# Where the gates of an output projection stand in an attention block on one Trainium2 core, with two roundings on GpSimd and two stores on ScalarE's queue

## The chip, the core and the metric

The kernel runs on one core of a Trainium2 chip. The core has five engines, each with its own queue of instructions, executed in order: TensorE (PE, with PEld for its weight loads), VectorE (DVE), ScalarE (ACT), GpSimd (POOL) and SyncE (SP, which here only issues transfers). An engine that meets an instruction whose input is not there waits, and everything behind it on that engine waits too. Metric is the device time of one execution in microseconds (us). Before the change it is 1550.36 us (median of three runs, 1550.10 to 1550.55).

## The reference

`x` is 2048 tokens by 512 channels. It is normalised by row; one branch is attention with 32 heads of 16 channels and an output projection `wo`, the other a two-layer network whose output passes through SiLU; the result is `x + s * g`.

```
xn = layernorm(x)
q, k, v = split(xn @ wqkv)                 # 32 heads of 16
p = softmax(q @ k.T * 16**-0.5)
s = concat_heads(p @ v) @ wo
h = gelu(xn @ w1 + b1) @ w2 + b2
g = silu(h)                                # = 0.5 * h * (1 + tanh(h / 2))
out = x + s * g
```

All is float32. Products that need the accuracy are made of three matrix multiplications of rounded parts: a number is split into a high part (rounded, `oh`, `wo_h`) and the rest (`ol`, `wo_l`), and high x high, low x high and high x low are added up in PSUM.

## The kernel before

The first part of the program makes the projections and the second branch; it writes `h` to DRAM as `g_d`. The main part is a list of 512 **steps**, n = 0 to 511, and a step 512 that closes it. Head groups (8 of 4 heads) and query chunks (4 of 512 tokens) make 32 units of 16 steps. A step takes 128 keys: four matrix multiplications of scores (`T` in the order strings, line 714, banks `ps`, `two` twice, `pst`), their three exponentials on ScalarE (lines 717 and 719), and the multiplication with the values (`V`, line 785, bank `pv`). Up to step 492 the steps also hold the row maxima of later units (`S`, `X`, `Y`: line 193 on TensorE, line 199 on VectorE).

From step `DONE = 493` the maxima are over, and their three PSUM banks (`ps_a`, `ps_b`, `ps_x`, handed out in turn by `s_tile`) serve the output projection, the **Wo part**. It takes tokens in blocks of 128. Blocks 0 to 9 go in **pairs** (0,1), (2,3) ... (8,9), each pair in four steps n to n+3, with n = 493, 497, 501, 505, 509. For a pair there are:

- `load_gx` (lines 841, 842): `g_d` and `x` of a block into `gx`, by SyncE's queue;
- `w_two` (lines 884 to 896), twice for a pair: 128 x 512 values of the attention output are rounded to `oh` (line 890 on ScalarE, or 892 on GpSimd), and GpSimd makes `ol` (line 893);
- `w_halves` (line 912, `H` in the order strings): the multiplications with `wo`, eight pieces in four steps. The pair's first piece needs two banks; of the three, one is free, and the other is that of the first block of the pair before;
- `gate` (lines 844 to 847): tanh on ScalarE into a scratch tile, then `g * (1 + tanh)` on VectorE, in place in `gx`. Scratch tile is number t % 4 of `home(0)`, so blocks 2 and 10, 4 and 12, 6 and 14 share one;
- `w_out` (`W` in the order string, step n+3): `w_gate` on VectorE (line 918) multiplies the bank with the gate and so frees the bank, `w_add` on GpSimd (line 923) adds `x`, and a transfer on SyncE's queue stores the block.

Blocks 10 to 15 (`late`) only get their gates there, one at every second step from 499 on; their projection follows after the last step. There the last unit's output is divided by its softmax sums: `os` is copied from PSUM, `dr` (the sums) is fetched from it, its reciprocal goes to DRAM (`den_d`, line 814), comes back spread over the rows (`dn`, line 817), and `o_div` multiplies (line 823). Then come the last rounding and the last multiplications.

The order of each engine's queue is the order in which the program is recorded: step by step, in a step by the letters of `ORDER` or `TWO`, and what `at(n, f, ...)` has put on a step is recorded behind its last `T`. Two steps of the Wo part run `TTTTHH` (odd n) and `HTTTTHWV` (even n).

Of the kernel before, what the change touches and what calls it, by code (L numbers as in the profile page):

```python
# [16 lines left out]
P = 128  # L17
# [37 lines left out]
def fused(ctx: ExitStack, tc: tile.TileContext, x, wqk, wv, wo, w1, b1, w2, b2, out):  # L55
    nc = tc.nc
# [254 lines left out]
    for j in range(len(pairs)):  # L311
        for h in range(2):
# [9 lines left out]
            n = 2 if nd < len(parts) and parts[nd][2] and ready - nd > room else 1  # L322
            n = max(n, need - 2 * (left - 1))
# [496 lines left out]
    def o_div(u, eng):  # L820
        g, c = divmod(u, NCH)
        rs = slice(64 * (g % 2), 64 * (g % 2) + 64)
        eng.tensor_mul(ot[c][rs, g // 2], ot[c][rs, g // 2], DN.pop(u)[rs])

    GX, OTS, PW, homes = {}, {}, {}, {}
# [23 lines left out]
    def w_round(blocks, src, lo):  # L849
        if blocks == [(t, KT - 1) for t in T3]:  # L850
            both = slot(3 + len(PN) % 3, (P, 4, KT, P), F32R)
            oh, ol = both[:, 0], both[:, 1]
        else:
            oh = wb.tile([P, KT, P], F32R, name="oh", bufs=3)
            ol = wb.tile([P, KT, P], F32R, name="ol", bufs=3)
        n = len(blocks)
        nc.scalar.activation(oh[:, :n], src, AF.Copy)
        lo.tensor_sub(ol[:, :n], src, oh[:, :n].bitcast(F32))
        for i, b in enumerate(blocks):
            OTS[b] = (oh[:, i], ol[:, i])  # L860
# [5 lines left out]
    def w_chunk(k, lo):  # L866
        w_round([(t, k) for t in T3], ot[NCH - 1][:, k].rearrange("p (t s) -> p t s", s=P), lo)

    def cols(t):
        n = 2 if t == NT - 1 else 1  # L870
        return [slice(i * D // n, (i + 1) * D // n) for i in range(n)]

    def w_mul(t, ks, parts=(0, 1)):
        if t not in PW:
            PW[t] = [t_bank(3 if t == NW else 2 if t == NW + 1 else 1) if NW <= t < NT - NCH or i else
                     ps_m.tile([P, CH], F32, name="ps") if t == NT - 1 else s_tile()[0]
                     for i, cs in enumerate(cols(t))]
        for i, cs in enumerate(cols(t)):
            if i in parts:
                for k in ks:  # L880
                    mm3(PW[t][i][:, :cs.stop - cs.start], OTS[t, k], (wo_h[:, k, cs], wo_l[:, k, cs]),
                        k == 0, k == KT - 1)

    def w_two(t, k0):
        oh, ol = [wb.tile([P, KT, P], F32R, name=x, bufs=3) for x in ("oh", "ol")]
        c, i = divmod(t, NCH)
        src = ot[c][:, k0:k0 + 2, i * P:(i + 2) * P]
        hi, lo = [w.rearrange("p (k t) s -> p k (t s)", t=2) for w in (oh, ol)]
        if t or k0:
            nc.scalar.activation(hi, src, AF.Copy)  # L890
        else:
            nc.gpsimd.tensor_copy(hi, src)
        nc.gpsimd.tensor_sub(lo, src, hi.bitcast(F32))
        for k in range(2):
            for j in range(2):
                OTS[t + j, k0 + k] = (oh[:, 2 * k + j], ol[:, 2 * k + j])
# [24 lines left out]
    def w_add(t, eng, i=0):  # L921
        gx, cs = GX[t], cols(t)[i]
        eng.tensor_add(gx[:, 0, cs], gx[:, 0, cs], gx[:, 1, cs])
        nc.sync.dma_start(out[t * P:(t + 1) * P, cs], gx[:, 0, cs])

    def w_out(t, eng):
        w_gate(t)
        w_add(t, eng)
# [3 lines left out]
    def at(n, f, *a, pos=3):  # L932
        todo.setdefault((n, pos), []).append((f, a))
# [27 lines left out]
    late = range(NW, NT)  # L961
    for t in range(NW):
        n = DONE + 4 * (t // 2)
        at(n - 3 + t % 2, load_gx, t)
        if t % 2 == 0:
            for i in range(2):
                at(n + i - 2, w_two, t, 2 * i)
            for i in range(4):
                for j in range(2):
                    at(n + i, w_halves, t, i % 2 * 2 + j, i // 2, pos="H")  # L970
        at(n + t % 2, gate, t)
        at(n + 3, w_out, t, nc.gpsimd, pos="W")
    for i, t in enumerate(late):
        n = L - 2 * len(late) - 1 + 2 * i
# [10 lines left out]
    for n in range(L + 1):  # L985
        ua, ka = divmod(n, 16)
        want = due(n) - due(n - 1)
        i = 0
# [42 lines left out]
            w_mul(t, (k,))  # L1031
    o_div(NU - 1, nc.vector)
    w_chunk(KT - 1, nc.vector)
    for t in T3[:2]:
        w_mul(t, KS[2:3])
    ends = [(t, i) for t in T3 for i in range(len(cols(t)))]
    for n, (t, i) in enumerate(ends):
        w_mul(t, KS if t == NT - 1 else KS[2:] if t == T3[2] else KS[3:], (i,))
        w_gate(t, i)
        w_add(t, nc.vector, i)  # L1040
# [33 lines left out]
```

## Time and profile before

| | |
|---|---|
| median of three runs | 1550.36 us |
| the profiled execution | 1550.88 us |
| its span (first to last instruction) | 1549.1 us |
| TensorE busy | 1541.8 us |
| VectorE busy | 1416.0 us |
| ScalarE busy | 1211.8 us |
| GpSimd busy | 366.4 us |
| the Wo part, step 493 to the values of step 511 | 1467.4 to about 1527 us |

The time line gives start and length of an instruction in us, engine, source line, operation, result and inputs, shape; "x2" are two merged; in brackets stands how long the engine had been idle and what ended that. DMA issues stand under the queue that issues them (SPq, ACTq). In the stage table each stretch has, for each engine, busy time and number of instructions, then TensorE's granted clock (1.00 is full), the busy share of the transfer engines, and GB/s.

### The profile page before, as it was taken

The page shows a single profiled execution, that of the slowest core. Times are in us where ns is not written, and L with a number is a line of the kernel's source. Part 1 is how long each engine was busy: PE and PEld are TensorE (multiplying, and loading weights), DVE is VectorE, ACT ScalarE, POOL GpSimd, SP SyncE. Part 2 cuts the span into 40 slices and gives each one's busy share as a digit, 9 for nine tenths or more (in the row PEclk, how much of TensorE's full clock was granted, in tenths as well). Part 3 has the DMA queues.
Part 4 walks back from the last instruction along what each step waited for, and adds up shares of the span by engine and source line. Part 5 has one row for each costly group of instructions (what it writes and reads, how often), then busy time and mean ns, then how long its engine had stood idle before and what let it go on. Part 6 is the DMA issues. An engine that isn't in the chain of part 4 may idle for free.

```text
span 1549.1 us, 31305 instructions
## 1 busy us (share of the span) xinstructions
PE 1541.8 (100%) x12240; PEld 923.4 (60%) x12240; DVE 1416.0 (91%) x2295; ACT 1211.8 (78%) x1881; POOL 366.4 (24%) x370
## 2 busy tenths in 40 slices
PE   9999999999999999999999999999999999999998
PEld 8889999989994444444444444444444444444456
DVE  7599999999998999999999999999999999999845
ACT  4333433333339999999999999999999999999984
POOL 4245675765741001002000100100010000000143
PEclk9999999999999999999999999999999999999999
DMA  6625443454422114113311411411041111110163
GB/s 211 154 60 144 132 141 101 138 159 120 133 85 76 44 30 73 30 36 61 64 32 32 70 36 37 66 37 29 23 81 29 34 30 32 42 30 22 46 198 117
DMA packets 78643, 116.83 MB, mean 75 GB/s; under 512 B 28036, under 2 KB 28292, under 8 KB 77320
## 3 DMA queue, kind: packets, MB, share of 16 engines
q1 hardware_dynamic: 74748, 101.89, 24.4%
q0 software_dynamic: 3264, 12.35, 4.7%
q8 instruction: 96, 1.57, 0.4%
q10 hardware_dynamic: 484, 0.60, 0.1%
q14 instruction: 51, 0.42, 0.1%
HBM read 84.35 MB, written 25.97 MB: 71 GB/s over the span
## 4 chain that ended last, share of the span: by engine, by line
PE 97%; DMA 1%; DVE 1%; ACT 0%; SPq 0%; POOL 0%; issue 0%; DVEq 0%; POOLq 0%
PE pv L785 32%; PE ps L193 22%; PE ps L583 13%; PE two L714 8%; PE sp L583 5%; PE pst L714 4%; PE ps L714 4%; PE pst L583 2%; PE pv L583 2%; PE ps L912 1%; PE ps L455 1%; PE ps L92 1%; PE pv L487 1%; DMA den_d<-dr 0%; DMA dn<-den_d 0%; DMA gx<-g_d 0%
## 5 line engine op out<-in xcount | busy, mean ns | idle before, releaser
L199 DVE TENSOR_REDUCE mx<-ps 128x2 f32<-128x512 f32 x2048 | 1317.4, 687 | 74.4 <-PE ps L193 25.6
L785 PE MATMUL pv<-slot,vsb 128*32 128x512 f32 x4096 | 543.4, 604 | 0.0
L719 ACT ACTIVATE slot<-two 128x1024 f32<-128x1024 f32 x511 | 520.1, 1018 | 0.1
L193 PEld LDWEIGHTS ps<-kt,slot 48*128 48x128 f32 x1362 | 212.8, 184 | 295.4 <-DVE mx L199 283.4
L193 PE MATMUL ps<-kt,slot 48*128 48x256 f32 (+1 forms) x1362 | 376.5, 365 | 0.0
L717 ACT ACTIVATE slot<-ps 128x512 f32<-128x512 f32 x515 | 307.6, 598 | 17.0 <-PE ps L714 7.0
L717 ACT ACTIVATE slot<-pst 128x512 f32<-128x512 f32 x511 | 308.9, 604 | 0.6 <-PE ps L714 0.6
L583 PE MATMUL ps<-slot,w1h 64*128 64x512 f32 x1088 | 224.9, 392 | 0.0
L193 PE MATMUL ps<-kt,qz 48*128 48x512 f32 x512 | 202.0, 394 | 0.0
L714 PE MATMUL two<-qt,kt 50*128 50x512 f32 x766 | 198.3, 395 | 0.7 <-ACT slot L719 0.4
L714 PE MATMUL ps<-qt,kt 50*128 50x512 f32 x387 | 189.9, 492 | 0.1
L193 PEld LDWEIGHTS ps<-slot,slot 48*128 48x128 f32 x594 | 93.2, 184 | 126.7 <-DVE mx L199 121.6
L193 PE MATMUL ps<-slot,slot 48*128 48x256 f32 (+1 forms) x594 | 165.2, 365 | 0.0
L785 PEld LDWEIGHTS pv<-slot,vsb 128*32 128x32 f32 x4096 | 81.5, 108 | 132.3 <-issue 124.4
L583 PEld LDWEIGHTS ps<-slot,w1h 64*128 64x128 f32 x1088 | 153.8, 185 | 9.8
L583 PE MATMUL ps<-slot,w1l 64*128 64x512 f32 x544 | 158.0, 392 | 0.0
L714 PE MATMUL pst<-qt,kt 50*128 50x512 f32 x383 | 156.0, 407 | 0.0
L375 POOL TENSOR_TENSOR hl<-hg,hh 128x512 fp32r<-128x512 f32 x76 | 96.7, 1295 | 153.1 <-ACT hh L374 107.6
L368 ACT ACTIVATE hg<-ps,b_sb 128x512 f32<-128x512 f32 x44 | 27.9, 685 | 134.1 <-PE ps L583 116.0
L714 PEld LDWEIGHTS two<-qt,kt 50*128 50x128 f32 x766 | 115.2, 185 | 1.8 <-ACT slot L719 0.7
L246 POOL CAST mh<-nt 128x32 fp32r<-128x32 f32 x19 | 4.0, 210 | 382.6 <-DVE nt L244 355.1
L193 PEld LDWEIGHTS ps<-kt,qz 48*128 48x128 f32 x512 | 93.7, 183 | 0.9 <-DVE mx L199 0.6
(194 smaller groups left out, 1962.5 us busy)
## 6 DMA issues: line engine op xcount, KB each, us to landing
raw<-in_w SPq DMA_DIRECT2D x88, 256.0 KB
qk_h<-hh SPq DMA_DIRECT2D x32, 256.0 KB
qk_l<-hl SPq DMA_DIRECT2D x32, 256.0 KB
qt<-qk_h SPq DMA_DIRECT2D x128, 64.0 KB
slot<-qk_h SPq DMA_DIRECT2D x92, 64.0 KB
g_d<-gt POOLq DMA_DIRECT2D x16, 256.0 KB, 3.6
qt<-qk_l SPq DMA_DIRECT2D x64, 64.0 KB
dn<-den_d SPq DMA_DIRECT2D x32, 128.0 KB
```

Source lines behind the costliest of these rows:

```text
L92: nc.tensor.matmul(ps, lhs[a], rhs[b], start=first and n == 0, stop=last and n == 2)
L193: return nc.tensor.matmul(ps[:, c0:c0 + w], QS[u][r, p, qi * P:(qi + 1) * P], kts[u // NCH % KB][p][r, k0:k0 + w], start=True, stop=True).ins
L199: nc.vector.tensor_reduce(MX[u][:, 2 * p:2 * p + 2, qi, ki][:, heads, parts], ps.rearrange("p (n c) -> p n c", c=HC), axis=AX.X, op=OP.max)
L368: nc.scalar.activation(raw, ph.pop(u), AF.Gelu_apprx_tanh, bias=b1_sb[:, u[2]:u[2] + 1])
L375: nc.gpsimd.tensor_sub(hl, raw, hh.bitcast(F32))
L455: nc.tensor.matmul(pq["q", g, c], W1[g][i][:, k * P:(k + 1) * P], (xh, xl)[j][c][:, k], start=n == 0 and k == 0, stop=n == 2 and k == KT - 1)
L487: nc.tensor.matmul(pw[:, :P], ident, ident, start=True, stop=True)
L583: i = nc.tensor.matmul(ps, lhs[r], rhs[r], start=first, stop=last).ins
L714: nc.tensor.matmul(ps, kts[g % KB][p][r, k * P:(k + 1) * P], QT[u][r, p, :], start=True, stop=True)
L717: nc.scalar.activation(PT[u, k][:, 2 * p + a, :], ps, AF.Exp, scale=SCALE)
L719: nc.scalar.activation(PT[u, k][:, :2], TP["two"], AF.Exp, scale=SCALE)
L785: nc.tensor.matmul(PV[u][32 * j:32 * j + 32, :], vsb[:, k, h:h + 32], PT[u, k][:, j, :], start=(k == 0), stop=(k == NT - 1))
```

## The change

Four things are changed.

- The gates of a pair move from its first two steps (n and n+1) to its last two (n+2 and n+3). `w_out` stays at n+3, and the gates of the late blocks stay where they were.
- The two `w_two` of the first pair move from steps 491 and 492 to steps 486 and 488.
- The second of them is rounded by GpSimd like the first; before, ScalarE did it.
- The stores of blocks 10 and 11, which SyncE issued behind their additions, are issued by ScalarE's queue, behind the last rounding of the tail.

```diff
@@ w_two
-        if t or k0:
+        if t:
             nc.scalar.activation(hi, src, AF.Copy)
         else:
             nc.gpsimd.tensor_copy(hi, src)
@@ w_add
         eng.tensor_add(gx[:, 0, cs], gx[:, 0, cs], gx[:, 1, cs])
-        nc.sync.dma_start(out[t * P:(t + 1) * P, cs], gx[:, 0, cs])
+        if t not in late[:2]:
+            w_store(t, nc.sync, i)
+
+    def w_store(t, eng, i=0):
+        cs = cols(t)[i]
+        eng.dma_start(out[t * P:(t + 1) * P, cs], GX[t][:, 0, cs])
@@ the steps of a pair
-                at(n + i - 2, w_two, t, 2 * i)
+                at(n + i - 2 if t else n + 2 * i - 7, w_two, t, 2 * i)
...
-        at(n + t % 2, gate, t)
+        at(n + 2 + t % 2, gate, t)
         at(n + 3, w_out, t, nc.gpsimd, pos="W")
@@ the tail
     w_chunk(KT - 1, nc.vector)
+    for t in late[:2]:
+        w_store(t, nc.scalar)
```

ScalarE's queue in steps 499 and 500, the last two of pair (2,3). L717 and L719 are the exponentials, L890 is the rounding of a `w_two`, L846 a tanh; `gx_20200` and `gx_20232` (after: `gx_20195` and `gx_20230`) are blocks 2 and 3, `kt0` holds block 10. Before, from the tanh of block 3 in step 498 on:

```order
L846 ACTIVATE slot0_20159<-gx_20232 128x512
L717 ACTIVATE slot4_20363<-ps_20364 128x512
L719 ACTIVATE slot4_20363<-two_6832 128x1024
L717 ACTIVATE slot4_20363<-pst_20374 128x512
L890 ACTIVATE oh_20377<-slot7_6843 128x512
L846 ACTIVATE slot0_20159<-kt0_20235 128x512
L717 ACTIVATE slot5_20408<-ps_20409 128x512
L719 ACTIVATE slot5_20408<-two_6832 128x1024
L717 ACTIVATE slot5_20408<-pst_20415 128x512
L890 ACTIVATE oh_20418<-slot7_6843 128x512
```

The same two steps after:

```order
L717 ACTIVATE slot4_20359<-ps_20360 128x512
L719 ACTIVATE slot4_20359<-two_6832 128x1024
L717 ACTIVATE slot4_20359<-pst_20370 128x512
L846 ACTIVATE slot0_20223<-gx_20195 128x512
L890 ACTIVATE oh_20375<-slot7_6843 128x512
L846 ACTIVATE slot0_20223<-kt0_20233 128x512
L717 ACTIVATE slot5_20406<-ps_20407 128x512
L719 ACTIVATE slot5_20406<-two_6832 128x1024
L717 ACTIVATE slot5_20406<-pst_20413 128x512
L846 ACTIVATE slot0_20223<-gx_20230 128x512
L890 ACTIVATE oh_20418<-slot7_6843 128x512
```

The tanhs of blocks 2 and 3 now stand in these two steps, each ahead of a rounding, and the steps behind them (501, 502) have none but that of a late block.

VectorE's queue from the same place on. L847 is the second half of a gate, L918 is `w_gate`, which frees a bank, L792 the copy of a unit's output, L813 the reciprocal of its sums. Before:

```order
L792 COPY os_20291<-pv_19839 128x512
L847 SCALAR_TENSOR_TENSOR gx_20200<-slot0_20159,gx_20200 128x512
L847 SCALAR_TENSOR_TENSOR gx_20232<-slot0_20159,gx_20232 128x512
L813 RECIPROCAL dr_20297<-dr_20297 128x16
L847 SCALAR_TENSOR_TENSOR kt0_20235<-slot0_20159,kt0_20235 128x512
L918 SCALAR_TENSOR_TENSOR gx_20200<-ps_20313,gx_20200 128x512
L918 SCALAR_TENSOR_TENSOR gx_20232<-ps_20314,gx_20232 128x512
```

After:

```order
L792 COPY os_20291<-pv_19839 128x512
L813 RECIPROCAL dr_20297<-dr_20297 128x16
L847 SCALAR_TENSOR_TENSOR gx_20195<-slot0_20223,gx_20195 128x512
L847 SCALAR_TENSOR_TENSOR kt0_20233<-slot0_20223,kt0_20233 128x512
L847 SCALAR_TENSOR_TENSOR gx_20230<-slot0_20223,gx_20230 128x512
L918 SCALAR_TENSOR_TENSOR gx_20195<-ps_20311,gx_20195 128x512
L918 SCALAR_TENSOR_TENSOR gx_20230<-ps_20312,gx_20230 128x512
```

The second half of block 3's gate now stands directly ahead of both `w_gate`; before, an earlier step's work stood there.

GpSimd's queue around the first pair's `w_two`. L892 and L893 are rounding and rest, L246 and L247 belong to the row maxima, L823 is `o_div`:

```order
 L892 CAST oh<-slot_6842 128x512
 L893 TENSOR_TENSOR ol<-slot_6842,oh 128x512
-L246 CAST mh<-nt 128x32
-L247 TENSOR_TENSOR mh<-nt,mh 128x32
+L892 CAST oh<-slot_6842 128x512
 L893 TENSOR_TENSOR ol<-slot_6842,oh 128x512
+L246 CAST mh<-nt 128x32
+L247 TENSOR_TENSOR mh<-nt,mh 128x32
 L823 TENSOR_TENSOR slot_6843<-slot_6843,dn 64x512
```

The second rounding and its rest now stand directly behind the first, ahead of the work on the maxima.

## The prediction

> **What bounds the kernel now.** I read the page first, then the table by stage for the Wo part (one stretch for each two steps), then the time line where a stretch is longer than its neighbours, and last the end of the program.
>
> ```profile
> PE 1541.8 (100%) x12240; PEld 923.4 (60%) x12240; DVE 1416.0 (91%) x2295; ACT 1211.8 (78%) x1881; POOL 366.4 (24%) x370
> ...
> 1467.36:1473.90 6.54, 6.39 (x53) 3.68 (x50) 2.63 (x5) 5.97 (x11) 3.00 (x4) 1.00 0.10 14
> 1473.90:1479.68 5.78, 5.78 (x52) 3.44 (x48) 1.85 (x3) 5.04 (x8) 1.39 (x2) 1.00 0.83 263
> ...
> 1485.48:1491.27 5.79, 5.79 (x52) 3.38 (x49) 2.90 (x5) 5.26 (x9) 1.29 (x1) 1.00 0.60 184
> ...
> 1497.06:1504.34 7.28, 6.79 (x52) 3.47 (x49) 2.85 (x4) 5.55 (x10) 2.57 (x2) 1.00 0.91 286
> ...
> 1515.92:1521.72 5.80, 5.80 (x53) 3.36 (x50) 2.44 (x3) 5.45 (x10) 3.80 (x3) 1.00 0.26 96
> ```
>
> The nine stretches from 1467.36 to 1521.72 are steps 493 to 510, two each. TensorE is busy in all of an ordinary one: 5.79 us are its own work, so any time it waits there is added to the end. ScalarE has 5.0 to 5.7 us of work in each. Two stretches are longer: the first (steps 493, 494) by 0.75, and that of steps 503, 504 by 1.49. I call the start of an odd step's scores T; the stretches begin there (steps 493, 495, ... 511 at 1467.36, 1473.90, ... 1521.72).
>
> **The first pair's roundings.** They go to GpSimd's idle time.
>
> ```profile
> 1434.46 0.61 POOL L892 CAST oh<-slot 128x512 fp32r<-128x512 f32 x1
> 1469.10 1.30 POOL L893 TENSOR_TENSOR ol<-slot,oh 128x512 fp32r<-128x512 f32 x1
> ...
> 1468.05 0.62 PE L912 MATMUL ps<-wo_h,oh 64*128 64x512 f32 x2
> 1470.45 0.50 PE L912 MATMUL ps<-wo_h,ol 64*128 64x512 f32 x2 [0.15 <-POOL ol L893]
> 1470.79 0.39 PE L714 MATMUL ps<-qt,kt 50*128 50x512 f32 x1
> ...
> 1474.46 0.40 PE L912 MATMUL ps<-wo_h,oh 64*128 64x512 f32 x2
> 1476.55 0.40 PE L714 MATMUL ps<-qt,kt 50*128 50x512 f32 x1
> ```
>
> GpSimd ran the first rounding at 1434.46, a long way ahead of its step, because it waits for data alone; the second, one more 0.61 and 1.30 us, will run right behind it and beside a VectorE that reads maxima from PSUM. Today the second rest starts at 1469.10 and TensorE waits for it at 1470.45. From the first Wo piece to the next scores it takes 1470.79 - 1468.05 = 2.74 us there, against 1476.55 - 1474.46 = 2.09 in the next pair. Gain: 0.65. (The other 0.10 of that stretch lies ahead of the first piece and stays.)
>
> **The late load.** In steps 501 to 504 a gate waits for its input.
>
> ```profile
> 1494.65 0.45 SPq L841 DMA_DIRECT2D gx<-g_d  x1
> 1498.79 0.63 ACT L846 ACTIVATE slot<-gx 128x512 f32<-128x512 f32 x1 [2.06 <-DMA gx<-g_d]
> ```
>
> The tanh of block 5 (step 502) waits 2.06 us for a load that SyncE issued at 1494.65; the exponentials behind it are late, and the stretch is 1.49 longer. The change puts this tanh into step 504, some 6 us later, and the load can hardly be more than 1 us later. Gain: 1.49.
>
> **The gates, where I see the cost.** Now `w_gate` stands on VectorE behind the gate of the pair's second block, which needs the tanh of step n+3, which stands behind that step's exponentials. The next pair's first Wo piece needs the bank that `w_gate` frees. The prices:
>
> ```profile
> 1485.48 0.50 PE L714 MATMUL ps<-qt,kt 50*128 50x512 f32 x1
> 1486.01 0.60 ACT L717 ACTIVATE slot<-ps 128x512 f32<-128x512 f32 x1 [0.71 <-PE ps L714]
> 1487.89 0.64 ACT L890 ACTIVATE oh<-slot 128x512 fp32r<-128x512 f32 x1
> 1488.41 0.64 ACT L846 ACTIVATE slot<-kt 128x512 f32<-128x512 f32 x1
> 1488.93 0.61 ACT L717 ACTIVATE slot<-ps 128x512 f32<-128x512 f32 x1
> 1490.79 0.67 ACT L890 ACTIVATE oh<-slot 128x512 fp32r<-128x512 f32 x1
> ...
> 1484.66 0.64 ACT L846 ACTIVATE slot<-gx 128x512 f32<-128x512 f32 x1
> 1485.34 0.69 DVE L847 SCALAR_TENSOR_TENSOR gx<-slot,gx 128x512 f32<-128x512 f32 x1 [1.42 <-ACT slot L846]
> 1477.94 1.29 DVE L918 SCALAR_TENSOR_TENSOR gx<-ps,gx 128x512 f32<-128x512 f32 x2 [3.49 <-PE ps L912]
> ```
>
> From T, the exponentials start at 0.53; the first small instruction behind them at T+2.41 (1.88 later); each small one takes 0.52 of the queue; the even step's three exponentials take 1.86. A tanh is 0.64, VectorE follows after 0.04 with 0.69, and one `w_gate` is 0.65. The next pair's first piece wants its bank at 5.79 + 0.56 = T+6.35 (0.56 is 1474.46 - 1473.90).
>
> Pair (0,1), T in step 495: two small instructions (tanh, rounding) end at T+3.45, exponentials at 5.31, tanh of block 1 at 5.95, its gate at 6.68, `w_gate` at 7.33. TensorE waits until about 7.35: 1.0 us.
>
> Pairs (2,3), (4,5), (6,7), T in steps 499, 503, 507: a late block's tanh is the third small instruction, and it uses the same scratch tile as the pair's first gate (2 and 10, and so on), so it must wait for that gate: tanh 2.41 to 3.05, gate to 3.78, late tanh from 3.82. The exponentials then start at 4.34, the tanh at 6.20, the gate at 6.88, and `w_gate` ends at 8.22. TensorE waits until about 8.25: 1.9 us, three times.
>
> Today the two `w_gate` run from 1477.94 to 1479.23, at once behind the last Wo piece, and the next pair's first piece comes about 1 us later, at 1480.2 by the same 0.56: no wait. Bounds for one such wait: none, if TensorE had other work to put there (it has not, its queue is in order), and 2.5, if GpSimd also held VectorE up:
>
> ```profile
> 1506.08 2.55 POOL L923 TENSOR_TENSOR gx<-gx 128x512 f32<-128x512 f32 x2
> 1507.48 1.69 DVE L847 SCALAR_TENSOR_TENSOR gx<-slot,gx 128x512 f32<-128x512 f32 x1 [2.50 <-ACT slot L846]
> ...
> 1531.08 0.69 DVE L923 TENSOR_TENSOR kt<-kt 128x512 f32<-128x512 f32 x1
> 1531.33 1.59 POOL L858 TENSOR_TENSOR ol<-ot,oh 128x512 fp32r<-128x512 f32 x1 [2.66 <-ACT oh L857]
> ```
>
> A gate that meets a GpSimd instruction lasts until 0.54 after that one's end (1508.63, 1509.17); one that began first keeps its 0.69, and GpSimd's takes 0.3 more. In steps 495 to 508 the pair's gates begin ahead of GpSimd's rest (rounding done at T+3.57 and 7.36, gates begun at 3.09 and 6.88), so I take 1.0 and three times 1.9, 6.7 in all. TensorE gets to step 511 by 6.7 - 0.65 - 1.49 = 4.56 later.
>
> What moves with it at no cost: the ten tanhs and ten gates are the same in number; each rounding slips by 0.52, its rest ends at T+4.9 and 8.75 (0.08 after the rounding, then 1.3), and the third Wo piece, which needs the second, comes 1.4 behind the first (two thirds of 2.09), at 9.6. The exponentials of the even step end at 6.35 instead of 5.8, so the third of the next scores' banks is 0.2 late, inside the longer wait. The copy `os` of the unit that ends in step 495 stands behind the first pair's `w_gate` and slips by 1.4 us, with its transfers; their user is the rounding of step 507, 25 us on. SyncE issues the stores of a pair 2 to 3 us later, and behind them loads whose gates now come two steps later. If one of these covers fails, the cost is that of the late load of today, 1.5.
>
> **The tail.** Pair (8,9) has its gates in steps 511 and 512, just ahead of the copy `os` from which the last chain runs.
>
> ```profile
> 1527.45 1.58 SPq L924 DMA_DIRECT2D out<-gx  x2
> 1527.58 0.42 DVE L795 COPY os<-pv 128x256 f32<-128x256 f32 x1 [1.00 <-ACT os L794]
> 1528.04 1.14 ACTq L805 DMA_DIRECT2D dr<-os  x1
> 1529.13 1.16 SPq L808 DMA_DIRECT2D ot<-os  x2
> 1530.72 0.33 SPq L814 DMA_DIRECT2D den_d<-dr  x1
> 1532.94 0.58 SPq L817 DMA_DIRECT2D dn<-den_d  x1
> 1537.66 0.69 DVE L823 TENSOR_TENSOR ot<-ot,dn 64x512 f32<-64x512 f32 x1 [2.36 <-DMA dn<-den_d]
> ...
> 1429.09 0.59 SPq L817 DMA_DIRECT2D dn<-den_d  x1
> 1433.11 1.29 POOL L823 TENSOR_TENSOR slot<-slot,dn 64x512 f32<-64x512 f32 x1 [3.03 <-DMA dn<-den_d]
> ```
>
> From T = 1521.72: `os` is complete today at T+6.3, `den_d` issued at 9.0. After: tanh of block 8 at 2.41, GpSimd's rest at 3.75 to 5.04, tanh of block 9 ends at 4.09, and here its gate meets GpSimd and ends at 5.04 + 0.55 = 5.6; two `w_gate` to 6.9, `os` complete at 7.3, 1.0 later. GpSimd's two additions (2.55) follow the first `w_gate` and end at 8.8; the second store, two `ot` transfers (1.16) and then `den_d` leave SyncE's queue at about 10.45: 1.45 later than today. Against it stands the load `dn`: today 4.72 us from its issue to its user, with two stores issued right behind it; at 1429.09 it took 4.02 with none. ScalarE now issues them when `dn` has been used and nothing stands behind them on its queue; on SyncE's queue the next work is block 12's store, and nobody waited for these two: gain 0.7. They still end well ahead of the last store, which is issued some 8 us after that rounding begins. Tail: +0.75, with 0 (SyncE's wait hidden) and 1.5 (no gain on `dn`) as ends.
>
> **The sum.** 4.56 + 0.75 = 5.3 us: on the profiled execution's own 1550.88 that is 1556.2; the median of the runs stands 0.5 lower, so 1555.7.
>
> **The rivals.**
> - The waits are not what ends last. If TensorE lost nothing at the four seams, the two gains of 2.14 and the tail's 0.75 would leave 1.4 less, 1549.0: not slower. For it speaks that ScalarE, which sets the gates, has 0.5 us to spare in a stretch; against it that the tanh stands behind exponentials that cannot start before TensorE's scores. It decides where the seams cost less than 0.35 us each.
> - The seams are cheaper by half, since the late tanh does not wait for the scratch tile (0.38 less at three seams) or VectorE is quicker: 1.5 to 3 less, 1552.7 to 1554.2.
> - TensorE's clock falls at each of its waits. By the rows it would run two steps at half clock, 5.79 more after each of four seams: 23 us, 1579; for one step of the two 1567. A wait of 0.6 us did not lower it:
>
> ```profile
> 1538.00:1540.00 2.00, 1.39 (x5) 0.52 (x5) 1.04 (x2) 0.63 (x1) 0.00 (x0) 1.00 0.01 4
> ```
>
>   The Trainium skill ("TensorE: Matmul & The Clock Gate", Part 1, "The HAM clock gate", and "A second HAM failure mode: psum-queue depth-cycling") says that an idle window of about 3.4 us halves the clock, and also that frequent short idling between groups on PSUM banks can make it swing. By the first rule the sum stays as it is; by the second it would be this rival's. The trace agrees with the first as far as its one gap goes, and no row has waits of 1.9 us.
> - The moved loads and stores turn late: SyncE's stores of a pair come 2 to 3 us later, and block 8's load waits for block 4's store. It would then miss step 511's gate; by my times it lands some 10 us ahead, so I give this little.
>
> **How the numbers follow.** The forecast with its own bounds (seams of 0.7 and thrice 1.6, to 1.2 and thrice 2.2; tail 0 to 1.5) is 1553.3 to 1557.6: 0.76. Half-priced seams below 1553.3: 0.08, half of it within 0.2%. Nothing lost at the seams: 0.09, mostly within 0.2%, a third of it faster. The clock: 0.04. Late transfers, 1558 to 1560: 0.03. About 0.2%, 3.1 us, is what a measurement here tells from no change; so faster 0.04, same 0.10, slower 0.86. The range 1552.8 to 1557.6 holds 0.8.
>
> **What would show it.** Right: in the stage table the stretch of steps 493, 494 falls to 5.9, that of 503, 504 no longer has the load's wait, and the stretches of steps 497, 501, 505 and 509 are 1.0, 1.9, 1.9, 1.9 longer, with TensorE's L912 idle behind VectorE's L918; `den_d` is issued about 10.4 us after the last T, and `dn` takes 4.0. Wrong: L912 without such a wait, a new wait of an L846 for `gx`, or a granted clock below 1.00.

## The result, and the profile after

The changed kernel takes 1558.03 us (median of five runs, 1556.46 to 1558.44), the kernel before beside it 1550.51 (1550.10 to 1550.65): ratio 1.0048, 95% interval 1.0037 to 1.0058. It is slower, by 7.5 us; 1555.7 had been forecast, with 1557.6 as the upper end of the range.

The profiled execution after took 1558.03 us with a span of 1556.2. The stage table of the changed kernel, steps 493 and 494 first, two steps a stretch (columns: stretch, its length, then busy time and number of instructions of PE, PEld, DVE, ACT and POOL, granted TensorE clock, share of the transfer engines, GB/s):

```profile
1467.21:1473.33 6.12, 6.12 (x53) 4.03 (x50) 1.03 (x3) 4.54 (x8) 1.75 (x3) 1.00 0.06 16
...
1479.12:1486.00 6.88, 6.28 (x52) 3.48 (x48) 2.49 (x4) 4.59 (x8) 3.78 (x3) 1.00 0.24 87
...
1491.79:1499.55 7.76, 6.64 (x53) 3.57 (x50) 2.60 (x4) 5.99 (x11) 4.34 (x4) 1.00 0.39 104
1499.55:1505.34 5.79, 5.79 (x53) 3.35 (x49) 1.70 (x2) 4.97 (x9) 2.44 (x2) 1.00 0.88 278
1505.34:1514.74 9.40, 8.22 (x53) 4.81 (x49) 2.64 (x4) 6.03 (x11) 4.25 (x3) 0.82 0.75 250
...
1520.53:1528.39 7.86, 6.70 (x53) 3.62 (x49) 2.65 (x4) 6.56 (x12) 4.36 (x4) 1.00 0.18 68
```

The stretch of steps 503 and 504 (the fourth row) has lost the load's wait: 5.79 instead of 7.28. The four stretches in which a pair follows a pair are 1.09, 1.97, 3.61 and 2.07 longer than 5.79, and in the third of them the mean granted clock is 0.82. The time line shows TensorE's wait at each of these four seams:

```profile
1480.68 0.49 PE L912 MATMUL ps<-wo_h,oh 64*128 64x512 f32 x1 [0.60 <-DVE gx L918]
1494.23 0.49 PE L912 MATMUL ps<-wo_h,oh 64*128 64x512 f32 x1 [1.12 <-DVE gx L918]
1507.88 0.79 PE L912 MATMUL ps<-wo_h,oh 64*128 64x512 f32 x1 [1.18 <-DVE gx L918]
1523.08 0.49 PE L912 MATMUL ps<-wo_h,oh 64*128 64x512 f32 x1 [1.17 <-DVE gx L918]
```

Before, no Wo piece waited for `w_gate` (L918). The chain behind the second of them, in steps 499 and 500 of the changed kernel, from ScalarE's and VectorE's time lines:

```profile
1489.09 0.69 DVE L847 SCALAR_TENSOR_TENSOR gx<-slot,gx 128x512 f32<-128x512 f32 x1 [2.76 <-ACT slot L846]
...
1489.82 0.63 ACT L846 ACTIVATE slot<-kt 128x512 f32<-128x512 f32 x1 [0.24 <-DVE gx L847]
1492.21 0.64 ACT L846 ACTIVATE slot<-gx 128x512 f32<-128x512 f32 x1
1492.88 0.69 DVE L847 SCALAR_TENSOR_TENSOR gx<-slot,gx 128x512 f32<-128x512 f32 x1 [1.40 <-ACT slot L846]
1493.49 1.28 DVE L918 SCALAR_TENSOR_TENSOR gx<-ps,gx 128x512 f32<-128x512 f32 x2
```

It is the chain that the prediction laid out: block 10's tanh waits for block 2's gate to leave the scratch tile, block 3's tanh follows the exponentials, its gate follows the tanh, and the two `w_gate` follow the gate. TensorE goes on at 1494.23, that is T + 8.23, against 8.25 forecast.

What had been given a chance of 0.04 is, for one seam, in the third. Every fall of the clock in the Wo part, here and below, lasts 3.41 us, and in the one profile that has two they begin 30.72 us apart, nine times 3.413 (1496.40 and 1527.12, in the kernel with one copy more, below); so the clock is counted here in such periods. The first row is the period of the changed kernel that holds the wait of the second seam; the two behind it are the period with the wait of the third seam and the one that follows, all in the stage table's columns:

```profile
1490.82:1494.23 3.41, 2.29 (x17) 0.72 (x10) 2.01 (x4) 3.41 (x7) 0.90 (x2) 1.00 0.32 106
...
1504.47:1507.88 3.41, 2.23 (x17) 0.67 (x9) 1.95 (x4) 3.41 (x7) 0.90 (x2) 1.00 0.86 238
1507.88:1511.30 3.42, 3.42 (x16) 2.76 (x18) 1.29 (x2) 1.49 (x3) 3.41 (x3) 0.50 0.81 302
```

And two rows of TensorE's time line in the last of them, then the same two of the second profile (a run without a fall, below):

```profile
1508.91 1.05 PE L912 MATMUL ps<-wo_h,oh 64*128 64x512 f32 x2
1509.33 1.04 PE L912 MATMUL ps<-wo_l,oh 64*128 64x512 f32 x2
```

```profile
1508.15 0.62 PE L912 MATMUL ps<-wo_h,oh 64*128 64x512 f32 x2
1508.39 0.62 PE L912 MATMUL ps<-wo_l,oh 64*128 64x512 f32 x2
```

TensorE stood idle for 1.18 us of the period from 1504.47, and for the whole of the next the clock was 0.50; the period from 1490.82 has 1.12 us of idle time, nearly the same work, and full clock behind it. At 0.50, pairs of pieces start 0.42 apart, at full clock 0.24. That is the 1.5 us by which this seam exceeds its neighbours. Not every run has such a fall, which is why the runs lie further apart than those of before.

### The profile page after: what moved, and what is told of

Same layout as the page of the kernel before. It is cut to its first block, busy times and chain, and to the rows that moved or that the text cites. A ratio compares the mean times of both kernels' runs of the same rounds, so it can differ in the third digit from the quotient of the medians.

```text
span 1556.2 us, 31306 instructions
## 1 busy us (share of the span) xinstructions
PE 1545.6 (99%) x12240; PEld 927.5 (60%) x12240; DVE 1411.8 (91%) x2295; ACT 1211.5 (78%) x1880; POOL 368.4 (24%) x371
## 3 DMA queue, kind: packets, MB, share of 16 engines
q10 hardware_dynamic: 772, 1.12, 0.2%
## 4 chain that ended last, share of the span: by engine, by line
PE 94%; DMA 2%; DVE 1%; issue 1%; SPq 1%; POOL 1%; ACT 0%; POOLq 0%; DVEq 0%
PE pv L785 32%; PE ps L193 22%; PE ps L583 13%; PE two L714 7%; PE sp L583 5%; PE pst L714 4%; PE ps L714 4%; PE pst L583 2%; PE pv L583 2%; PE ps L455 1%; DMA out<-gx 1%; PE ps L92 1%; DMA den_d<-dr 0%; DMA dn<-den_d 0%; DMA gx<-g_d 0%
## 5 line engine op out<-in xcount | busy, mean ns | idle before, releaser
L719 ACT ACTIVATE slot<-two 128x1024 f32<-128x1024 f32 x511 | 520.0, 1018 | 0.0
L717 ACT ACTIVATE slot<-ps 128x512 f32<-128x512 f32 x515 | 307.5, 598 | 26.2 <-PE ps L714 12.6
L717 ACT ACTIVATE slot<-pst 128x512 f32<-128x512 f32 x511 | 308.9, 604 | 0.6 <-PE ps L714 0.6
L246 POOL CAST mh<-nt 128x32 fp32r<-128x32 f32 x19 | 4.0, 211 | 386.3 <-DVE nt L244 358.4
```

Source lines behind the costliest of these rows:

```text
L246: nc.gpsimd.tensor_copy(mh[:, 0], nt)
L717: nc.scalar.activation(PT[u, k][:, 2 * p + a, :], ps, AF.Exp, scale=SCALE)
L719: nc.scalar.activation(PT[u, k][:, :2], TP["two"], AF.Exp, scale=SCALE)
```

## The experiments

Two theories were set against rivals. Theory S: the loss is made at the seams, where the next pair's first piece waits for a bank that `w_gate` frees late. Theory C, formed after the result: the granted clock falls because TensorE stands idle there. All times are medians; the kernel before, run beside each group, took 1550.29, 1550.27 and 1550.20.

### The gates alone

```diff
 # the kernel before
-        at(n + t % 2, gate, t)
+        at(n + 2 + t % 2, gate, t)
```

> Before, with the gates of a pair moved to its last two steps and nothing else. Theory S (seams: w_gate stands behind the last gate, and the next pair's first Wo piece waits for its bank): four seams of 1.1, 2.0, 2.0 and 2.1 us, the late load's 1.5 gone, a tail 1.2 longer, so 6.9 above before, 1557.4 us; and 1559.0 where TensorE's clock falls for one window. Theory P (the roundings or the stores carry a good part of the loss): less than 4 above before.

Measured 1557.95 (1557.46 to 1559.33), ratio 1.0050 (1.0037 to 1.0062). The gates alone make the whole loss. Four runs with a mean clock of 1.000 lie at 1557.46 to 1558.12 and the one with 0.999 at 1559.33, where 1557.4 and, with a fall, 1559.0 had been expected. The profiled execution had no fall of the clock, so this is the third seam by itself:

```profile
1505.93:1513.80 7.87, 6.70 (x54) 3.69 (x50) 2.66 (x4) 6.04 (x11) 4.28 (x3) 1.00 0.61 200
```

It is 2.08 longer than 5.79. The changed kernel's 3.61 is thus 2.1 of waiting and 1.5 of clock.

### Everything but the gates

```diff
 # the changed kernel
-        at(n + 2 + t % 2, gate, t)
+        at(n + t % 2, gate, t)
```

> After, with the gates back in a pair's first two steps: the roundings on GpSimd and the two stores on ScalarE's queue stay. Theory S: 0.6 gained at the first pair and 0.7 to 1.1 at the load dn, 1.3 to 1.7 below before, 1549.0 us; no seam, granted clock 1.00 throughout. Theory P: no gain, or a loss of over 1 us.

Measured 1549.84 (1549.15 to 1550.43), ratio 0.9996 (0.9987 to 1.0005): the roundings and the stores cost nothing, and their gain is not clear of the noise. In the profile it is there. The first stretch is 6.10 long instead of 6.54, and in the tail `dn` takes 4.04 us from its issue to its user instead of 4.72, as it did before where no stores stood behind it (rows of the time line):

```profile
1532.88 0.58 SPq L817 DMA_DIRECT2D dn<-den_d  x1
1536.92 0.69 DVE L823 TENSOR_TENSOR ot<-ot,dn 64x512 f32<-64x512 f32 x1 [1.64 <-DMA dn<-den_d]
```

Together 1.1 us; the medians show 0.45. The Wo part began 0.44 later in this profiled execution than in the one of before (other profiles have it up to 0.4 earlier or later), which no part of the change explains.

### The gates one step later only

```diff
 # the changed kernel
-        at(n + 2 + t % 2, gate, t)
+        at(n + 1 + t % 2, gate, t)
```

> After, with the gates of a pair in its second and third step (n+1 and n+2). Theory S: both gates end over 1 us ahead of the pair's last Wo piece, so w_gate waits for TensorE alone and the seams are gone; the gains of 0.6 (first pair) and 0.7 to 1.1 (dn) stay, and most of the late load's 1.5, since the tanh of block 5 now comes at about 1499 us, when its load lands: 1547.6 us. Theory A (ScalarE is overfull where a pair's gates share steps with the next pair's roundings and a late block's tanh): half of the crowding stays, 2 to 3 above before.

Measured 1548.97 (1548.44 to 1550.33), ratio 0.9992 (0.9984 to 1.0001). No seam is left, as S says, but 1.4 us of the hoped-for gain are missing too. A late load has taken 1.05 of them again, one block on. ScalarE's time line:

```profile
1500.85 0.63 ACT L846 ACTIVATE slot<-slot 128x512 f32<-128x512 f32 x1 [0.85 <-DMA slot<-g_d]
```

The stretch behind it in the stage table:

```profile
1502.14:1508.98 6.84, 6.54 (x52) 3.72 (x48) 2.18 (x5) 6.56 (x11) 4.24 (x3) 1.00 0.85 295
```

The tanh of block 12 (step 503) now waits for its own load, issued at 1495.39 behind the same `dn` as block 5's. In the changed kernel the same load is issued at 1496.74, and the tanh that uses it starts at 1503.41 without waiting for it: the seams have made the user later by 2.56 and the load by 1.35.

### The banks first, the gates after

```diff
 # the changed kernel
         nc.scalar.activation(e, g, AF.Tanh, scale=0.5)
+        if t >= NW:
+            gate_mul(t)
+
+    def gate_mul(t):
+        e, g = home(0)[:, t % NCH], GX[t][:, 0]
...
-        at(n + 3, w_out, t, nc.gpsimd, pos="W")
+        if t % 2:
+            for f in (w_gate, gate_mul):
+                for s in (t - 1, t):
+                    at(n + 3, f, s, pos="W")
+            for s in (t - 1, t):
+                at(n + 3, w_add, s, nc.gpsimd, pos="W")
```

> After, ScalarE's queue unchanged: the tanhs stay in a pair's last two steps, but VectorE multiplies the bank with half of g first (w_gate) and with 1 + tanh after it, so the bank is free without the tanh. The result is the same. Theory S: the four seams are gone, TensorE has 5.79 us in each stretch of two steps, 1547.5 to 1548.5 us, and the granted clock is 1.00. Theory A (ScalarE's crowding delays the next scores): the seams stay at half of their length or more, 1553 us or more.

The tanhs stay where the change put them, but the bank is multiplied with `g` first and with `1 + tanh` afterwards, so that no bank waits for a tanh. (Contrary to the expectation's "The result is the same", blocks 2, 4 and 6 get another block's gate in this kernel, because the tanh of the late block overwrites the shared scratch tile before it is used.) Measured 1552.62 (1551.39 to 1554.16), ratio 1.0016 (1.0007 to 1.0025). No Wo piece waits for `w_gate` any more, as S said: the stretches that begin with steps 497, 501 and 509 are 5.79, 6.15 and 6.14 long. But the time is 4 to 5 us above the expectation. In the profiled execution (1553.74) 3.4 us stand in the stretches of steps 503 and 505, 6.53 and 8.49 long where 5.79 is the ordinary length; there block 12's tanh waits even longer for its load (ScalarE's time line):

```profile
1502.70 0.63 ACT L846 ACTIVATE slot<-slot 128x512 f32<-128x512 f32 x1 [1.79 <-DMA slot<-g_d]
```

The clock falls right behind it, as two of its periods show in the stage table's columns:

```profile
1502.84:1506.26 3.42, 2.34 (x15) 1.23 (x13) 1.73 (x3) 3.42 (x7) 0.00 (x0) 1.00 0.70 250
1506.26:1509.67 3.41, 3.41 (x18) 2.67 (x18) 2.67 (x4) 2.71 (x5) 2.71 (x2) 0.50 0.94 309
```

Seven of the eleven runs have a mean clock of 1.000, at 1551.39 to 1554.16, so without a fall the kernel is late too; what makes up the rest was not taken apart. In this kernel and in the one before it, then, the change's gain on the late load (1.49) passes on, in whole or in part, to the next load in the queue.

### A scratch tile of its own for the late block

```diff
 # the changed kernel
-        e, g = home(0)[:, t % NCH], GX[t][:, 0]
+        e, g = home(0)[:, (t + (t >= NW)) % NCH], GX[t][:, 0]
```

> As the changed kernel, but a late block's tanh writes the scratch tile beside the pair's, so that it does not wait for the pair's first gate. Theory S (the chain tanh, gate, w_gate behind the exponentials sets each seam): the waits of 0.24 to 0.30 us that the late tanh had go, and the seams of steps 501, 505 and 509 are some 0.3 shorter each: 0.9 less in all, 1555.7 in runs at full clock (1557.3 where the clock falls once). Rival (VectorE or the bank's order sets the seam, not ScalarE's queue): no change, 1556.6 and 1558.1.

Measured 1555.78 (1555.63 to 1556.26), ratio 1.0035 (1.0022 to 1.0047). The second seam's stretch:

```profile
1491.75:1499.16 7.41, 6.31 (x53) 3.54 (x50) 2.60 (x4) 5.65 (x10) 4.23 (x3) 1.00 0.47 126
```

It is 0.35 shorter than the changed kernel's, the 0.24 of the late tanh's wait and a little more. The late tanh's place in ScalarE's queue is part of what sets the seam: S holds, and its rival (no change) falls.

### One copy more ahead of `w_gate`

```diff
 # the changed kernel
     def w_out(t, eng):
+        if t < NW and t % 2 == 0:
+            nc.vector.tensor_copy(home(0)[:, (t + 1) % NCH], PW[t][0])
```

> As the changed kernel, with one more VectorE copy of a bank into a scratch tile ahead of each pair's first w_gate: some 0.65 us longer at each of the four seams and in the tail. Theory S: 3.2 us more, 1559.8 at full clock. Theory C (the clock falls by the length of the wait): waits of 1.7 to 2.6 us now lower it in every run and at more than one seam, each for 3.41 us at a price of about 1.6, so 1561.5 to 1564.5. Rival N (by chance): 1559.8 to 1561.4 as before.

Measured 1563.84 (1563.36 to 1564.10), ratio 1.0086 (1.0072 to 1.0100). The second and the fourth seam in the stage table, and periods of the clock: the one with the second seam's wait, the one behind it, and the one behind the fourth seam's wait:

```profile
1492.29:1502.38 10.09, 8.18 (x54) 4.75 (x50) 3.65 (x5) 6.00 (x11) 5.52 (x4) 0.83 0.64 201
...
1522.62:1532.81 10.19, 8.22 (x54) 4.78 (x50) 3.71 (x5) 6.56 (x12) 4.84 (x4) 0.83 0.14 53
...
1492.98:1496.40 3.42, 1.50 (x11) 0.95 (x12) 2.67 (x5) 3.30 (x6) 2.12 (x2) 1.00 0.20 58
1496.40:1499.81 3.41, 3.41 (x20) 2.69 (x18) 0.99 (x1) 0.35 (x1) 3.33 (x3) 0.50 0.90 255
...
1527.12:1530.53 3.41, 3.41 (x20) 2.66 (x17) 0.70 (x1) 0.88 (x2) 1.83 (x2) 0.50 0.41 153
```

The first and the third seam are 7.67 and 8.66 long at full clock, 0.8 more than without the copy; the second and fourth have the same 0.8 and another 1.5 of clock. All four runs have a mean clock below 1 (0.997 to 0.999), and the time lies in C's range, above that of chance. The first and the third seam kept full clock behind waits of 1.39 and 1.97 us, the latter split between two periods of the clock (0.50 and 1.46).

### TensorE kept busy at the seams

```diff
 # the changed kernel, w_halves
                 PW[i] = [s_tile()[0]]
+            for _ in range((0, 4, 7, 7, 7)[t // 2]):
+                nc.tensor.matmul(PW[t][0], wo_h[:, 0, :P], wo_h[:, 0], start=True, stop=True)
```

> As the changed kernel, but TensorE is given 4 (first seam) and 7 (the others) multiplications of 128x128x512, 0.23 us each, whose result nobody reads, into the bank that is free while it waits for the other: 0.9 and 1.6 us, less than the waits of 1.1 and 2.0. Clock theory C (the granted clock falls because TensorE stands idle at the seam): the seams stay as long as they are, every run has full clock, and the median is 1556.6, none above 1557.3. Rival N (the fall has another cause, or comes by chance): it comes in about half of the runs as before, with a median of 1557.5 to 1558.4. If the added work delays the first piece, it is by at most 0.3 a seam, 1557.8 at full clock.

Measured 1558.29 (1557.90 to 1558.45), ratio 1.0050 (1.0036 to 1.0063), every run at full clock. But the added work was too long: it delays the first piece, and the second seam's stretch is 8.14. Both theories had a time near this one, so the time decides nothing, only the clock does. With less work, `(0, 3, 5, 5, 5)`:

> As the changed kernel, with 3 (first seam) and 5 (the others) unread multiplications instead of 4 and 7, which took 0.27 us each and delayed the first piece by 0.2 to 0.4 a seam: now 0.8 and 1.35 us, and no delay beyond 0.1. Clock theory C (the clock falls because TensorE stands idle at the seam): the same seams as in the changed kernel, full clock in every run, 1556.6 (1556.3 to 1557.1). Rival N (by chance, or for another cause): in about half of the runs 1.5 more, 1558.1.

Measured 1556.69 (1556.58 to 1558.24), ratio 1.0045 (1.0032 to 1.0057), every run at full clock; the second seam:

```profile
1491.55:1499.31 7.76, 7.76 (x59) 4.91 (x55) 2.62 (x4) 5.99 (x11) 5.52 (x4) 1.00 0.48 149
```

The stretch is as long as the changed kernel's, 7.76, but TensorE is busy in all of it. Four of five runs are within 0.3 of 1556.6, as C says; the fifth, 1558.24 at full clock, is explained by neither theory. Against the changed kernel run beside it (1557.22, next) the median is 0.5 lower, which is within the noise; what the two fillings show is ten runs of ten at full clock.

### The changed kernel again

> The changed kernel once more, beside these two, to count the runs in which the clock falls. Theory C (a wait of about 1.5 us lowers the clock in some runs, by where it lies against the clock's own 3.41 us periods): times in two groups, 1556.4 to 1556.8 and 1558.0 to 1558.5, and a profile with a fall begins it right behind one of the four seams. Rival N: falls elsewhere too, or times spread evenly.

Measured 1557.22 (1556.52 to 1557.92), ratio 1.0046 (1.0033 to 1.0058). With the first five these are ten runs, by mean granted clock:

| mean clock | runs, us | median | spans, first to last instruction |
|---|---|---|---|
| 1.000 | 1556.46, 1556.52, 1556.77, 1556.79, 1557.22, 1557.35 | 1556.8 | 1554.7 to 1555.4 |
| 0.999 | 1557.92, 1558.03, 1558.07, 1558.44 | 1558.1 | 1556.1 to 1556.6 |

The two groups are there, 1.3 apart. The lower one reaches higher than the 1556.8 expected, but the run of 1557.35 has a span of only 1554.8. A fall of 3.41 us to 0.50 takes 0.0011 off the mean (1.7 of 1556), so a mean of 1.000 rules one out; 0.999 does not prove one: a run with the scratch tile of its own has 0.999 and a profile without a fall in the Wo part. Four of ten is thus the most there can have been. This time the profiled execution had no fall. Its stage table:

```profile
1466.92:1473.02 6.10, 6.10 (x52) 4.01 (x48) 1.03 (x3) 4.53 (x8) 1.76 (x3) 1.00 0.06 14
...
1478.82:1485.69 6.87, 6.27 (x52) 3.52 (x48) 2.49 (x4) 4.59 (x8) 3.77 (x3) 1.00 0.22 83
...
1491.48:1499.25 7.77, 6.65 (x54) 3.60 (x50) 2.61 (x4) 5.99 (x11) 4.97 (x4) 1.00 0.51 128
1499.25:1505.04 5.79, 5.79 (x53) 3.37 (x49) 1.70 (x2) 4.96 (x9) 1.82 (x2) 1.00 0.87 312
1505.04:1512.90 7.86, 6.68 (x52) 3.61 (x49) 2.65 (x4) 6.04 (x11) 4.27 (x3) 1.00 0.64 214
...
1518.70:1526.55 7.85, 6.68 (x53) 3.74 (x50) 2.65 (x4) 6.54 (x12) 4.37 (x4) 1.00 0.18 68
```

TensorE's waits are as long as in the first profile: 0.60, 1.12, 1.18 and 1.17. What differs is where they lie against the clock's periods. In the first profile the third seam's 1.18 filled the end of one period; here they are split, 0.22 and 0.96:

```profile
1503.21:1506.63 3.42, 3.20 (x23) 1.03 (x21) 1.39 (x2) 3.42 (x7) 1.02 (x1) 1.00 0.90 269
1506.63:1510.04 3.41, 2.45 (x22) 2.01 (x24) 2.26 (x4) 2.45 (x5) 3.29 (x3) 1.00 0.58 212
```

That fits C, by which it depends on where a wait lies against these periods; it rests on one profile of each kind.

### The middle placing with the late gates moved

```diff
 # the changed kernel
-        at(n + 2 + t % 2, gate, t)
+        at(n + 1 + t % 2, gate, t)
...
-        at(n, gate, t)        # late blocks
+        at(n + 1, gate, t)
```

> As the changed kernel, but with a pair's gates in its second and third step (as in the middle placing tried before) and each late block's gate one step later, in an even step. No seam, since the second gate is done a step before w_gate; block 12's tanh comes some 3 us later than there, where it had waited 0.85 us for its load. If that load wait was what the middle placing still lost, the stretch of steps 503 and 504 falls from 6.84 to 5.8, and the time from 1548.97 to 1547.9, 2.4 below the kernel before. Rival: the wait goes to another block, 1548.9; or the three small ScalarE instructions make the scores' banks late, 1549.5.

Measured 1556.57 (1555.10 to 1558.82), ratio 1.0039 (1.0027 to 1.0052): a clear miss. (By mean clock: 1555.10 and 1555.56 at 1.000, 1556.57 and 1556.80 at 0.999, 1558.82 at 0.997, which would fit no fall, one and two. The profiled run is the 1555.10.) Three seams are back, 8.05 to 8.07 long, and the time line says why:

```profile
1490.87 0.67 ACT L846 ACTIVATE slot<-kt 128x512 f32<-128x512 f32 x1
...
1491.57 1.35 DVE L847 SCALAR_TENSOR_TENSOR kt<-slot,kt 128x512 f32<-128x512 f32 x1 [2.76 <-ACT slot L846]
1492.84 1.27 DVE L918 SCALAR_TENSOR_TENSOR gx<-ps,gx 128x512 f32<-128x512 f32 x2
1493.57 0.49 PE L912 MATMUL ps<-wo_h,oh 64*128 64x512 f32 x1 [1.78 <-DVE gx L918]
```

A late block's gate (`kt` is block 10) now stands in step n+3 ahead of `w_gate` on VectorE, and `w_gate` waits for its tanh although it has nothing to do with it. The expectation had looked at ScalarE alone. The miss supports S from another side: any gate in a pair's last step, its own or not, makes the seam.

The middle placing again, with only block 12's gate moved, from step 503 to 505:

```diff
 # the middle placing
-        at(n, gate, t)        # late blocks
+        at(n + 2 * (i == 2), gate, t)
```

> The middle placing (a pair's gates in its second and third step), with block 12's gate alone moved from step 503 to 505, where it stands behind no w_gate and its load has 5.8 us more. In the run with late gates one step later the seams came back, since a late gate then stood ahead of w_gate in VectorE's queue; theory S says that here there are none. The stretch of steps 503 and 504 falls from 6.84 to 5.8: 1.05 below the middle placing, 1547.9. Rival: another block's load or tanh is late instead, 1548.5 to 1549.

Measured 1548.13 (1547.95 to 1549.82), ratio 0.9989 (0.9980 to 0.9998). This version is ahead of both kernels, of the one before by 2.1 us, where the interval just excludes no change. Its stretch of steps 503 and 504 is like any other:

```profile
1502.80:1508.59 5.79, 5.79 (x53) 3.37 (x49) 2.12 (x2) 5.44 (x10) 3.79 (x3) 1.00 0.99 308
```

## Why the prediction was right or wrong

**Direction and mechanism: right.** The seams are there, at the four places named, with L912 idle behind L918; the gates alone bring the loss, and the rival in which the waits are not what ends last has fallen, with that of half-priced seams.

**The seams: right, a little low.** At full clock they cost 1.08, 1.98, 2.07 and 2.06 (the second profile of the changed kernel, against 5.79), 7.2 in all, where 1.0 and three times 1.9 had been put, 6.7. The moment at which TensorE goes on was met at the first and second seam (7.35 and 8.23 after T, 7.35 and 8.25 forecast) and missed by 0.08 and 0.09 at the others (8.33 and 8.34). Most of the 0.5 comes behind it: from the piece that waited to the next T it takes 5.32 (1494.23 to 1499.55), where the ordinary stretch has 5.23 (5.79 less 0.56), some 0.1 at each seam. The bounds were added up with a slip: 0.7 and three times 1.6, less 2.14, give 3.4 and thus 1553.7 as the lower end, not 1553.3, and the upper end comes to 1557.5; neither changes what follows.

**The first pair: too high.** The stretch became 6.10 to 6.12 long, not 5.9: a gain of 0.44 where 0.65 had been put. The wait for `ol` is gone, and TensorE is busy in all of the stretch. In the first profile it takes 2.20 from the first Wo piece to the next scores (1467.90 to 1470.10), 0.54 less than the 2.74 of before, but 3.23 from there to the next T instead of 3.11. Why the latter grew stays open.

**The late load: right in this kernel.** 7.28 became 5.79, 1.49 as forecast. The two runs without seams showed what the prediction had not seen: block 12's load stands two transfers behind block 5's, and its tanh is the next that waits. The prediction had asked about lateness for the moved loads and stores, not for the next load in the queue; that the seams covered it here was luck.

**The tail: right as a sum, wrong in its terms.** In the first profile after, from the last T to VectorE's last instruction, it is 0.5 longer, in the second 0.85; 0.75 had been put. The rows of the first:

```profile
1535.03 0.41 DVE L795 COPY os<-pv 128x256 f32<-128x256 f32 x1
...
1539.26 0.33 SPq L814 DMA_DIRECT2D den_d<-dr  x1
1541.23 0.58 SPq L817 DMA_DIRECT2D dn<-den_d  x1
...
1544.83 0.69 DVE L823 TENSOR_TENSOR ot<-ot,dn 64x512 f32<-64x512 f32 x1 [1.31 <-DMA dn<-den_d]
```

From T = 1528.39, `os` is complete at T + 7.05 (7.3 forecast), `den_d` is issued at T + 10.87 (10.45 forecast), and `dn` takes 3.60 (4.0 forecast).

**The clock: this step failed.** It stood among the rivals as "TensorE's clock falls at each of its waits", with two steps or one at half clock behind each of four seams (23 or 11.6 us) and a chance of 0.04, and it was left out of the sum. The evidence taken for leaving it out was one wait of 0.6 us. The runs show neither of the two forms: a wait of about 1.2 us can lower the clock for one period of 3.41 us, at a price of 1.5 us, in at most four of ten runs and, where it is seen, at one seam of four. It should have stood in the sum as a good chance of 1.5 us, which moves the upper end of the range to 1559.

By full clock the working comes out: in the second profile the Wo part grew by 59.63 - 54.36 = 5.3 us from step 493 to step 511 (4.6 forecast) and the tail by 0.85, 6.1 in all, on 1550.5; the six runs at full clock have 1556.8. The other 1.3 us to 1558.0 fit the clock's price. Without a fall the time would have lain inside the range, so which side of its end the median fell on was in part the luck of the runs; the sum itself was 1.1 low.

The Trainium skill ("TensorE: Matmul & The Clock Gate", Part 1, "The HAM clock gate") says that the clock is halved after at least one idle window of about 3.4 us, and that the window is free-running. The length of the period agrees with the trace, 3.41 us, and so does the free run: the third seam meets it at another point in each of the two profiles of the changed kernel. The idle window does not: TensorE was busy for 2.23 of the 3.41 us ahead of the fall.

## What to carry to other kernels

Before an instruction is moved later on an engine, list what stands behind it on the next engine in the chain, whether or not it needs the result: here a bank was held by a gate, and in one trial by another block's gate. Where a wait is removed, ask for the next user of the same queue; it may be one transfer behind. And a wait on TensorE can cost more than its length: here waits of 1.1 to 2 us were followed by half clock for a period of 3.41 us in a share of the runs, at 1.5 us each, so such a price belongs in the range.

## What the hardware showed that was not expected

The granted clock fell to 0.50 for one period of 3.41 us behind periods in which TensorE had still been busy for 1.45 to 2.34 us: after 1.18 us idle (changed kernel), 1.08 (banks first), 1.92 and 1.97 (one copy more). Idle time alone does not decide it. Periods with as much idle time as the first, or more, were followed by full clock, one in the profile of the scratch tile of its own (the first row) and others in that of the middle placing with late gates moved:

```profile
1504.15:1507.56 3.41, 2.23 (x19) 0.97 (x11) 2.36 (x4) 3.41 (x7) 1.30 (x3) 1.00 0.88 247
...
1492.15:1495.57 3.42, 2.00 (x18) 1.72 (x20) 1.97 (x3) 1.28 (x2) 2.19 (x3) 1.00 0.06 11
...
1519.46:1522.87 3.41, 1.63 (x15) 1.34 (x16) 2.34 (x3) 1.66 (x3) 2.18 (x3) 1.00 0.00 0
```

TensorE was idle for 1.18, 1.42 and 1.78 us here. The kind of work may count beside the idle time. Periods filled mostly with Wo pieces kept full clock behind 1.42 to 1.78 us idle and lost it behind 1.92 and 1.97 (one copy more); periods that held scores and value multiplications as well lost it behind 1.08 and 1.18 and kept it behind 1.12 and 1.18. That is argued from 13 profiles and was not tried; what decides a fall stays open. In the profiles without a TensorE wait above 0.5 us (before, both fillings, the middle placings without seams, everything but the gates) the clock did not fall in the Wo part.
